# Low parts of q and V in the first batch made on GpSimd, with V scaled on ScalarE

## The chip, the cores and the metric

The kernel runs on one core of a Trainium2 chip. The metric is the device time of one execution in microseconds. The core has five engines, each with an instruction queue of its own that it works off in order: TensorE (PE in the profile, with PEld for the loading of weights), VectorE (DVE), ScalarE (ACT), GpSimd (POOL) and SyncE (SP), which here only issues DMA transfers. An instruction whose input isn't there holds up everything behind it in its own queue, and nothing else directly.

## The reference

What is computed is an attention over 2 batches of 8 heads with 768 positions of 64 numbers, in which a query sees only the keys that fall in its bucket (the signs of six random projections), and behind it two MLP layers on the 1536 tokens:

```python
mask = q_bucket[:, :, :, None] == k_bucket[:, :, None, :]
scores = scale * np.matmul(q, k.transpose(0, 1, 3, 2))
scores = np.where(mask, scores, -1000000000.0)
scores = scores - np.max(scores, axis=-1, keepdims=True)
attn = np.exp(scores)
attn = attn / (np.sum(attn, axis=-1, keepdims=True) + 1e-09)
out = np.matmul(attn, v)
...
h = x @ w_in                                  # both MLPs, 512 -> 2048 -> 512
g = h * (1.0 / (1.0 + np.exp(-1.702 * h)))    # the second MLP: without the 1.702
y = g @ w_out
```

## The kernel before

**Two parts for a number.** TensorE multiplies rounded numbers, so the kernel writes each float32 operand as a high part (the rounded number) and a low part (what the rounding lost) and multiplies the parts. A low part is a subtraction, `x - high`, on 128 partitions by 384 or 768 numbers. It is these subtractions that the change moves.

**Stages.** The attention runs over 96 steps: 16 heads, six blocks of 128 queries each. The first 48 steps are the first batch (`stage[0] == 0`), the rest the second batch, beside which the first MLP already works on the first batch's tokens (`stage[0] == 1`). From about 410 us on only the MLPs are left. In the trace of before the first batch's steps lie between some 13 and 150 us.

**One step j.** PE makes the scores in PSUM (`scores`, L404 and L405), DVE takes them out with the row's minimum (`top`, tile `p`, L422), ACT takes the exponential (`exps`, L427), ACT or in two of five steps of the first batch DVE rounds it to the high part (`p_high`, tile `hl`, L438 and L436), POOL makes its low part (`p_low`, L442). For every two steps SP issues one DMA that transposes both parts (`p_turn`, `pt<-hl`, L448), and PE multiplies them with V three steps behind (`av`, L460 to L462). `p` has three buffers in the first batch, the scores two, `hl` three.

**Preparing the next pair of heads.** Between the steps the function `ahead` places the pieces that prepare a pair of heads. For q and k of a head: a load by SP (L268, one buffer for each of q and k); `natural`, which makes the high part on DVE (L292) and the low part (L293) on the engine that `LOWG` names; `turn`, which transposes both on PE (L300); `evict` and `move`, which put them in place. For the V of a pair: a load by SP (`load_v`, L279, one buffer), the maximum on DVE (`v_max`, L364), a scale from it (`v_spread`, `v_scale`), the high part on ACT with that scale (`v_high`, L383) and the low part (`v_low`, L389 to L392). The buffer of q, k or V can be loaded anew only when the low part that reads it is done.

`LOWG` is a pair of strings, one for each batch; a letter in it puts the low part of that tensor on GpSimd. In `natural` the first two heads (n of 0 and 1) stay on DVE whatever `LOWG` says; `v_low` has no such exception. What is prepared in the first batch reaches two pairs ahead, so `stage[0] == 0` covers q of heads 0 to 10 and V of pairs 0 to 4.

**What sets the order.** The kernel is written as a program over tiles. A list scheduler with a time model of its own puts the instructions of each engine in their order before the kernel runs; the offsets in `SOONER` bring a named piece forward. The semaphores follow from the tiles' reads and writes.

Of the kernel before, what the change touches and what calls it, by code (L numbers as in the profile page):

```python
# [21 lines left out]
def tile_lsh_attention_two_mlps(  # L22
# [44 lines left out]
    EARLY = 0  # L67
    WSTART = 38
    WEVERY = 3
    LOWG = ('k', 'kqv')  # L70
    COPY = ('k', 'q')
    FB = 2
    PB = 2
# [175 lines left out]
    def attention(sp, s1, ps_m, ps_v, ahead_of, setup):  # L249
# [37 lines left out]
        def natural(n, nm):  # L287
            x = nat[n, nm]
            hp, lp = (1, 0) if nm == "q" else (0, 1)
            E = G if nm in LOWG[stage[0]] and n > 1 else V  # L290
            t = sp.tile([P, NC, 2, D], F32R, tag="s" + nm, name="s" + nm, bufs=1)
# [93 lines left out]
        def v_low(pr, j):  # L385
            vs, s = st["v", pr]
            x = nat[pr, "v"][:, j]
            if "v" in LOWG[stage[0]]:
                A.activation(x, x, AF.Copy, scale=s[:, j:j + 1])  # L389
# [378 lines left out]
```

## Time and profile before

| what | value |
|---|---|
| time, median of 3 runs (lowest to highest) | 832.61 us (831.09 to 833.43) |
| the profiled execution's own time | 831.93 us |
| its span, first to last instruction | 830.1 us |
| mean granted TensorE clock | 0.955 |
| busy: PE, DVE, POOL, ACT | 753.3, 533.9, 442.0, 421.4 us |
| from 20 to 150 us, busy: DVE, PE, ACT, POOL | 104.69, 100.58, 89.77, 83.54 of 130 us |

The profile is of one execution. Busy time is given per engine and per stretch; waits name the engine and line that an idle engine was waiting for; the chain is the work that ended last, followed back from the end, each piece with its start and length. A busy PE is not PE at its peak, and spans on POOL are rough.

### The profile page before, as it was taken

The page shows a single profiled execution, that of the slowest core. Times are in us where ns is not written, and L with a number is a line of the kernel's source. Part 1 is how long each engine was busy: PE and PEld are TensorE (multiplying, and loading weights), DVE is VectorE, ACT ScalarE, POOL GpSimd, SP SyncE. Part 2 cuts the span into 40 slices and gives each one's busy share as a digit, 9 for nine tenths or more (in the row PEclk, how much of TensorE's full clock was granted, in tenths as well). Part 3 has the DMA queues.
Part 4 walks back from the last instruction along what each step waited for, and adds up shares of the span by engine and source line. Part 5 has one row for each costly group of instructions (what it writes and reads, how often), then busy time and mean ns, then how long its engine had stood idle before and what let it go on. Part 6 is the DMA issues. An engine that isn't in the chain of part 4 may idle for free.

```text
span 830.1 us, 13998 instructions
## 1 busy us (share of the span) xinstructions
PE 753.3 (91%) x5384; PEld 692.9 (83%) x5384; DVE 533.9 (64%) x932; ACT 421.4 (51%) x721; POOL 442.0 (53%) x345
## 2 busy tenths in 40 slices
PE   6787787698898998988999999979999999999998
PEld 5677576577797887887999999979999989998996
DVE  8877787988689889779424233899733843422222
ACT  6758656596675666655534232444645433321220
POOL 5656676777777857766733242549534533421120
PEclk9778979599999999999999999999999999999999
DMA  4999999998998979865587421232310400000112
GB/s 117 190 180 193 200 180 223 231 247 238 246 254 231 223 216 226 210 153 109 108 300 261 150 104 49 77 127 95 108 51 21 132 2 1 0 1 1 39 39 76
DMA packets 196270, 116.40 MB, mean 140 GB/s; under 512 B 153318, under 2 KB 175846, under 8 KB 196204
## 3 DMA queue, kind: packets, MB, share of 16 engines
q1 hardware_dynamic: 196044, 115.52, 55.8%
q8 instruction: 42, 0.69, 0.3%
q14 instruction: 24, 0.20, 0.1%
q10 hardware_dynamic: 160, 0.00, 0.0%
HBM read 56.63 MB, written 16.78 MB: 88 GB/s over the span
## 4 chain that ended last, share of the span: by engine, by line
PE 59%; DVE 20%; DMA 10%; ACT 5%; issue 4%; POOL 1%; SPq 1%; DVEq 0%; ACTq 0%; POOLq 0%
PE pso L642 26%; PE psh L608 25%; DMA pt<-hl 6%; DVE f L173 3%; DVE p L422 3%; DVE f L171 3%; DVE f L175 2%; DVE f L172 2%; PE pss L404 2%; PE pss L405 1%; PE psbit L332 1%; POOL hl L442 1%; DMA nk<-in_k_dram 1%; PE pav L460 1%; ACT p L427 1%
## 5 line engine op out<-in xcount | busy, mean ns | idle before, releaser
L619 POOL TENSOR_TENSOR gl<-g,gh 128x384 fp32r<-128x384 f32 x128 | 138.3, 1081 | 201.7 <-ACT gh L618 189.5
L442 POOL TENSOR_TENSOR hl<-p,hl 128x768 f16<-128x768 f32 x96 | 168.0, 1757 | 75.7 <-ACT hl L438 33.2
L608 PE MATMUL psh<-XH,wih 128*128 128x384 f32 x512 | 174.2, 340 | 6.0 <-DVE part L651 3.9
L608 PE MATMUL psh<-XH,wil 128*128 128x384 f32 x512 | 173.0, 338 | 0.0
L608 PE MATMUL psh<-XL,wih 128*128 128x384 f32 x512 | 172.9, 338 | 0.0
L617 DVE TENSOR_TENSOR g<-g,psh 128x384 f32<-128x384 f32 x96 | 52.7, 550 | 116.8 <-ACT g L616 116.7
L651 DVE SCALAR_TENSOR_TENSOR part<-pso,part 128x384 f32<-128x384 f32 (+1 forms) x124 | 72.6, 590 | 83.0 <-PE pso L642 82.8
L427 ACT ACTIVATE p<-p,lo 128x768 f32<-128x768 f32 x96 | 89.7, 937 | 70.4 <-DVE p L422 70.2
L618 ACT CAST gh<-g 128x384 fp32r<-128x384 f32 x128 | 65.5, 512 | 86.7 <-DVE g L617 70.7
L608 PEld LDWEIGHTS psh<-XH,wih 128*128 128x128 f32 x512 | 97.2, 190 | 8.1 <-DVE g L614 2.2
L642 PE MATMUL pso<-gh,woh 128*128 128x384 f32 x256 | 88.6, 352 | 16.9 <-DVE g L614 7.0
L422 DVE TENSOR_SCALAR_CACHE_REDUCE p<-pss 128x768 f32<-128x768 f32 x96 | 90.8, 947 | 14.9 <-PE pss L405 8.6
L608 PEld LDWEIGHTS psh<-XL,wih 128*128 128x128 f32 x512 | 97.2, 190 | 0.6
L608 PEld LDWEIGHTS psh<-XH,wil 128*128 128x128 f32 x512 | 97.2, 190 | 0.0
L616 ACT ACTIVATE g<-psh 128x384 f32<-128x384 f32 x96 | 46.8, 488 | 96.2 <-PE psh L608 95.2
L404 PE MATMUL pss<-ak,aq 128*128 128x384 f32 x192 | 77.4, 404 | 19.7 <-DVE p L422 19.5
L642 PE MATMUL pso<-gl,woh 128*128 128x384 f32 x256 | 86.5, 338 | 0.0
L642 PE MATMUL pso<-gh,wol 128*128 128x384 f32 x256 | 86.5, 338 | 0.0
L460 PE MATMUL pav<-VS,pt 128*128 128x65 f16 x576 | 69.4, 205 | 15.4 <-DMA pt<-hl 13.0
L460 PEld LDWEIGHTS <-pt 128*128 128x128 f16 x576 | 57.4, 105 | 24.1 <-DMA pt<-hl 17.7
L642 PE MATMUL pso<-woh,gh 128*128 128x512 f32 x192 | 74.9, 390 | 0.2 <-ACT gh L618 0.2
L642 PE MATMUL pso<-wol,gh 128*128 128x512 f32 x192 | 75.0, 391 | 0.0
(114 smaller groups left out, 1623.1 us busy)
## 6 DMA issues: line engine op xcount, KB each, us to landing
raw<-in_moe_w_in_dram SPq DMA_DIRECT2D x32, 512.0 KB
raw<-in_moe_w_out_dram SPq DMA_DIRECT2D x32, 512.0 KB
spih<-wih SPq DMA_DIRECT2D x13, 256.0 KB
spil<-wil SPq DMA_DIRECT2D x13, 256.0 KB
spoh<-woh SPq DMA_DIRECT2D x13, 256.0 KB
spol<-wol SPq DMA_DIRECT2D x13, 256.0 KB
wih<-spih SPq DMA_DIRECT2D x13, 256.0 KB
wil<-spil SPq DMA_DIRECT2D x13, 256.0 KB
```

The lines of the kernel that those rows point to most:

```text
L404: T.matmul(o, lhsT=lq, rhs=ak[:, half, :], start=True, stop=False)
L422: V.tensor_scalar(p, st.pop(("S", j)), LOW, None, op0=ALU.min, op1=ALU.min, accum_out=lo)
L427: A.activation(p, p, AF.Exp, bias=lo, scale=-1.0)
L442: G.tensor_tensor(out=hl[:, 1], in0=st.pop(("p", j))[0], in1=hl[:, 0], op=ALU.subtract)
L460: T.matmul(o, lhsT=pt[:, i], rhs=hv, start=(i == 0), stop=False)
L608: T.matmul(h, lhsT=a[:, c], rhs=x[t][:, c], start=(n == 0), stop=(n == 3 * NDC - 1))
L616: A.activation(g, h, AF.Sigmoid, scale=beta)
L617: V.tensor_tensor(out=g, in0=g, in1=h, op=ALU.mult)
L618: A.copy(gh[:, f], g)
L619: G.tensor_tensor(out=gl[:, f], in0=g, in1=gh[:, f].bitcast(F32), op=ALU.subtract)
L642: T.matmul(y, lhsT=a, rhs=x, start=(n == 0), stop=(n == 3 * nf - 1))
L651: V.scalar_tensor_tensor(out=acc, in0=y, scalar=scale, in1=acc, op0=ALU.mult, op1=ALU.add)
```

## The change

The first batch's entry of `LOWG` becomes the same as the second's. The constants' line is all of the diff:

```diff
-    LOWG = ('k', 'kqv')
+    LOWG = ('kqv', 'kqv')
```

By it two places of the code take their other branch in the first batch:

```python
E = G if nm in LOWG[stage[0]] and n > 1 else V          # natural, L290: now also for q
...
if "v" in LOWG[stage[0]]:                               # v_low, L388
    A.activation(x, x, AF.Copy, scale=s[:, j:j + 1])    # scale V in place on ScalarE
    G.tensor_tensor(out=vs[:, j, :, D + 1:], in0=x, in1=vs[:, j, :, 0:D], op=ALU.subtract)
else:
    V.scalar_tensor_tensor(out=vs[:, j, :, D + 1:], in0=x, scalar=s[:, j:j + 1],
                           in1=vs[:, j, :, 0:D], op0=ALU.mult, op1=ALU.subtract)
```

The low part of q of heads 2 to 10 is then a subtraction on GpSimd. The low part of V of pairs 0 to 4, two instructions for each pair, is no longer one DVE instruction that scales and subtracts but a scaling on ScalarE and a subtraction on GpSimd. Since the scheduler runs again, the order of other instructions can change with it.

## Rows read from the trace of the kernel before

**Rows 1.** The page: busy tenths of DVE, and DMA, in 40 slices of 20.75 us.

```profile
DVE  8877787988689889779424233899733843422222
DMA  4999999998998979865587421232310400000112
```

**Rows 2.** Busy time by stretch: length, engines (instructions), granted clock, DMA share, GB/s.

```profile
20.00:150.00 130.00, 100.58 (x1089) 86.72 (x1090) 104.69 (x198) 89.77 (x131) 83.54 (x54) 0.83 0.99 193
...
220.00:240.00 20.00, 17.25 (x152) 16.20 (x150) 18.85 (x34) 10.22 (x16) 15.00 (x11) 0.91 1.05 273
```

**Rows 3.** Groups by line, 20 to 150 us: count, busy us, mean ns, idle before.

```profile
L442 POOL TENSOR_TENSOR hl<-p,hl 128x768 f16<-128x768 f32 x45 | 76.3, 1708 | 38.1 <-DVE hl L436 23.6 <-ACT hl L438 10.3 <-issue 4.1
L422 DVE TENSOR_SCALAR_CACHE_REDUCE p<-pss 128x768 f32<-128x768 f32 x45 | 42.4, 945 | 2.3 <-POOL hl L442 1.6 <-PE pss L405 0.7
...
L392 DVE SCALAR_TENSOR_TENSOR VS<-nv,sv,VS 128x384 f16<-128x384 f32 x9 | 11.4, 1266 | 0.0
L293 POOL TENSOR_TENSOR sk<-nk,sk 128x384 fp32r<-128x384 f32 x9 | 9.3, 1031 | 8.5 <-DVE sk L292 6.1 <-PE pstr L300 1.6 <-DVE sv L378 0.4
...
L293 DVE TENSOR_TENSOR sq<-nq,sq 128x384 fp32r<-128x384 f32 x8 | 8.2, 1031 | 0.1
```

**Rows 4.** Waits of the engines, 20 to 150 us: us in total, times, longest.

```profile
ACT p L427 <- DVE p L422: 25.2, 16, 4.7
POOL hl L442 <- DVE hl L436: 23.6, 16, 4.3
...
PEld L460 <- DMA pt<-hl: 11.7, 9, 3.8
DVE am L364 <- DMA nv<-in_v_dram: 9.8, 4, 4.2
...
PE pstr L300 <- POOL sk L293: 2.9, 1, 2.9
```

**Rows 5.** Waits of SP, the DMA queue's own, in the same stretch.

```profile
SPq L448 <- POOL hl L442: 54.3, 20, 3.8
SPq L268 <- DVE sq L293: 3.2, 3, 2.2
```

**Rows 6.** The chain that ended last: start us, length us, engine, tile, line.

```profile
18.77 2.01 DVE VS L392 x2
...
25.70 0.89 DVE sq L293
...
58.44 0.76 DVE VS L392
...
61.81 1.66 POOL hl L442
...
89.55 1.15 DVE sq L293
...
103.09 1.27 DVE VS L392
...
134.12 1.98 POOL hl L442
```

**Rows 7.** Single lines, 20 to 150 us: ns least/median/most, first and last start.

```profile
L392 DVE SCALAR_TENSOR_TENSOR VS<-nv,sv,VS x9: 609/1218/2102, 19.1 to 133.5; 128x384 f16<-128x384 f32 x9
L436 DVE CAST hl<-p x18: 517/550/1387, 22.2 to 143.5; 128x768 f16<-128x768 f32 x18
L292 DVE CAST sq<-nq x8: 332/805/1642, 24.0 to 123.2; 128x384 fp32r<-128x384 f32 x8
L422 DVE TENSOR_SCALAR_CACHE_REDUCE p<-pss x45: 918/944/959, 21.3 to 147.5; 128x768 f32<-128x768 f32 x45
```

**Rows 8.** Groups by line over the whole run: the same pieces in the second batch.

```profile
L293 POOL TENSOR_TENSOR sq<-nq,sq 128x384 fp32r<-128x384 f32 x5 | 6.0, 1196 | 1.8 <-DVE sq L292 1.5 <-DMA BK<-ak 0.3
L390 POOL TENSOR_TENSOR VS<-nv,VS 128x384 f16<-128x384 f32 x6 | 6.8, 1151 | 2.4 <-ACT nv L389 2.4
L389 ACT ACTIVATE nv<-nv,sv 128x384 f32<-128x384 f32 x6 | 3.6, 620 | 0.0
```

## The prediction

> **What bounds the kernel now.** The change acts on the first batch alone, so I read that stretch and not the whole. First the slices of the page [rows 1]: the first seven (to 145 us) have DVE at seven to eight tenths with DMA at nine, and from about 400 us on neither is full. The windows say the same in numbers [rows 2]: of the 130 us from 20 to 150, DVE is busy 104.69 (81%), PE 100.58, ACT 89.77 and POOL 83.54 (64%), and the DMA engines' share is 0.99. No engine is full; DVE and the DMA engines are nearest to it. Who waits for whom then decides [rows 4]. The longest waits end on DVE: ACT waits 25.2 us for L422, and POOL 23.6 us for the high parts that DVE rounds. DVE itself loses 9.8 us in four waits for V's load. The other side is the DMA queue [rows 5]: SP, which works off its queue in order, waits 54.3 us in 20 waits for POOL's p_low before it can issue a transposing DMA, and PE's weight loads wait 11.7 us for those transposes [rows 4]. So there are two paths side by side: DVE makes the material, and POOL hands it to SP. The change takes load from the first and puts it on the second.
>
> **What leaves DVE.** In the stretch nine scale-and-subtract instructions for V (11.4 us) and eight subtractions for q (8.2 us) leave it, 19.6 us [rows 3], and one of each just ahead of it. That is their full weight as traced, locks included. What of it lies on the path? The chain [rows 6] holds five pieces of this work: 2.01 + 0.89 + 0.76 + 1.15 + 1.27 = 6.1 us. All other instances stand where DVE's queue had slack. I take 6.1 us as the gain; its bounds are 0 (another path just as long runs beside) and 19.6 (DVE sets the pace throughout).
>
> **What it costs on POOL.** q's subtraction on POOL took 1.196 us in the second batch and V's 1.151 [rows 8]; the like of it for k took 1.031 us in the first batch [rows 3]. Eight by 1.03 and nine by 1.15 is 18.6 us, which takes POOL from 83.5 to 102.1 of 130 us (79%). POOL idles 38.1 us ahead of L442 [rows 3], and an instruction that falls into this costs nothing. If that cover is gone, it holds up the p_low behind it, and SP with that. The chain passes p_low in five pieces with six instructions, 9.8 us together (first and last in [rows 6]). Seventeen new instructions on 45 p_lows are 0.38 for each; by 1.1 us and six this is 2.5 us if each holds up in full, and 0 if none does. I take half, 1.2 us. The natural order of the queue behind a new instruction is p_low, then SP's transpose, and behind that SP's loads of q, k and V, so a late p_low delays those too; that is the third rival below.
>
> **What it costs on ACT.** Nine scalings by 0.620 us [rows 8] are 5.6 us. ACT waits 25.2 us for L422 in the stretch [rows 4], and that wait hides them: 0, at worst 5.6 us if they always stand ahead of an exponential that could start.
>
> **What PE and the loads see.** The turn of q now waits for POOL. For k this was one wait of 2.9 us on the matrix side in nine low parts [rows 4]; the same for eight q would be 2.6 us, against 0 where the scheduler leaves room. I take 0.5, since PE has 29 us idle here [rows 2]. V's buffer comes free after 0.62 us on ACT and 1.15 on POOL in place of 1.27 on DVE, 0.5 us later each time; the next V load, and DVE's reduction that waits for it (9.8 us in four [rows 4]), come later by that: 2.0 us, or with a p_low of 1.7 us [rows 3] ahead in POOL's queue, 8.8 us; below, the reduction may be ordered later and wait less, by at most the 9.8 us that it waits now. I take 0.5 us, near the point where the scheduler puts the reduction behind the new landing time. The load of q is freed by POOL and no longer by DVE, for which SP now waits 3.2 us [rows 5]; I put that even.
>
> **What it does to the rest of DVE.** The spread of single lines [rows 7] shows that DVE's instructions don't have one duration: V's low part took 0.609 to 2.102 us, q's high part 0.332 to 1.642, while L422, which reads PSUM, stays within 0.918 to 0.959. The stretched ones are those that read SBUF while POOL works. With POOL busy 1.22 times as long, the excess on those that remain grows. For the eight casts of q the excess of the median over the least is 0.47 us, 3.8 us; with the casts of k, put as alike, 7.6 us; a growth by 0.22 is 1.7 us. In the proportion in which DVE's work lies on the chain (6.1 of 19.6) this is 0.5 us; bounds 0 and 1.7.
>
> The Trainium skill, SBUF — State Buffer, section "Who interferes with whom", speaks against the change here: DVE and GpSimd share a port pair under an exclusive lock, and a DVE instruction in a two-port mode or with two SBUF inputs is fully blocked until the GpSimd instruction that came first has ended. The rows agree as to which lines are stretched. By the rule alone each of the 35 remaining casts (18 and 17) would meet one of the new POOL instructions with a chance of about 0.14 and wait half of 1.1 us or more, an estimate of 2.7 us and not 1.7; on the chain 0.8 and not 0.5, which moves the forecast by 0.3 us.
>
> **What comes after.** From 160 us on PE, DVE and the weights are shared with the MLP, and DVE is busier still (18.85 of 20 us from 220 to 240 [rows 2]). `LOWG` of that batch is unchanged and its order follows the attention's, so I carry what the first batch gains or loses to the end one for one. The order of instructions may change anywhere, since the scheduler works anew; the trace can't price this. The nearest row is the wait for V's load, 9.8 us, which a better order would save and a worse one would double; I take 0 and keep both signs for the range.
>
> **The sum.** -6.1 (DVE) + 1.2 (POOL ahead of p_low) + 0 (ACT) + 0.5 (PE) + 0.5 (V's load) + 0.5 (locks) = -3.4 us. From the profiled execution's 831.9 this gives 828.5; the median of the runs shown is 0.7 us higher than that execution, so I put the time at 829.0.
>
> **Rivals.**
> DVE alone sets the pace: all of the 19.6 us less 1.7 for locks comes back, 831.9 - 17.9 = 814.0. For it speak the waits for L422; against it, that only 6.1 us of this work is on the chain and that a DMA share of 0.99 leaves no room for a stretch shorter by 14%.
> The DMA engines set the pace: the first batch stays as long as it is and the freed DVE time becomes longer waits for loads and for `pt<-hl`, 831.9 within 2.5 us. For it speaks the share of 0.99; against it, that SP waits 54.3 us for POOL, so transposes go out when they are made and not when the engines are free, and that 273 GB/s were moved from 220 to 240 us against 193 here [rows 2], with other transfers. The case in which the change does nothing it says, because too few pieces are covered, ends here too; the counts speak against it.
> POOL becomes the bound ahead of p_low (slower): SP's wait for p_low is the largest of all, and each new subtraction of 1.1 us that stands in front of a p_low whose high part is ready goes through SP to the transposes, the loads behind them and DVE's waits for those loads. The point from which it decides is six such instructions on the chain (6.1 / 1.1); with twelve of the seventeen it costs 13.2 us, and less the 6.1 that DVE gives the end is 831.9 + 7.1 = 839.0. For it speaks that POOL is the engine that SP waits for; against it, its 38.1 us of idle time ahead of p_low.
>
> **How the numbers follow.** A change of less than 0.3% (2.5 us) can't be told from none here. The forecast, partial relief of DVE, gets 0.43 and has a range of its own from 822 to 829.4. DVE alone gets 0.04, DMA as the bound or nothing 0.25, POOL as the bound 0.28. So faster is 0.47, within 0.3% 0.25, slower 0.28. The range must take in the second and most of the third rival, with some of the order's 9.8 us on both sides: 820 to 841. It leaves out DVE alone and the far end of POOL's case, together about 0.1.
>
> **What would show it.** In the profile of the changed kernel, from 20 to 150 us or where the first batch then ends: DVE's busy time lower by some 18 us and no L392 in it; POOL at about 102 us; L293 on POOL for q at 1.0 to 1.2 us; ACT's wait for L422 clearly below 25 us if DVE was the bound. If SP's wait for p_low rises over 54 us, or POOL's idle time ahead of L442 goes to a few us while ACT and DVE wait for POOL, the slower rival is right. If DVE's waits for the loads of q, k and V and PE's for `pt<-hl` grow by what DVE lost in work, it is the DMA. The prediction is wrong in its ground if the first batch keeps its length while the second changes, since I carry the one into the other unchanged.

## The result, and the profile after

The changed kernel takes 839.91 us (median; 836.88 to 840.64) against 832.55 for the kernel before: a ratio of 1.0083, with a 95% interval of 1.0055 to 1.0112. It is slower by some 7 us, where 829.0 was forecast. The profiled execution of after is the quickest of its four (836.88 us); its span is 835.0 us, against 830.1, so its trace shows some 5 us of the loss.

The stretches first, as in [rows 2]: length, then busy time and instructions of PE, PE's weight loads, DVE, ACT and POOL, then granted clock, DMA share and GB/s. The kernel after, most of the first batch and most of the second:

```profile
20.00:150.00 130.00, 95.76 (x1092) 80.39 (x1092) 88.35 (x178) 92.94 (x141) 98.98 (x72) 0.89 0.99 193
155.00:430.00 275.00, 241.30 (x2089) 220.31 (x2089) 225.05 (x376) 174.64 (x285) 188.90 (x136) 0.96 0.84 202
```

The second stretch of the kernel before:

```profile
155.00:430.00 275.00, 244.56 (x2113) 225.15 (x2114) 218.70 (x382) 176.16 (x291) 190.57 (x139) 0.96 0.86 210
```

In the first batch the load moved nearly as forecast: DVE is busy 88.35 us for 104.69, POOL 98.98 for 83.54, ACT 92.94 for 89.77. (PE's 95.76 for 100.58 goes with a granted clock of 0.89 for 0.83; where the first batch is that of before, this stretch had from 0.82 in other_nudge to 0.87 in old_work_new_second, so I don't count it to the change.) In the second batch, which the diff doesn't touch, DVE is busy 6.4 us longer and does six instructions fewer in the same 275 us, and PE runs 24 matmuls fewer. So the second stretch falls behind.

The moved work in the first batch of after (groups by line as in [rows 3]: count, busy us, mean ns, idle before):

```profile
L442 POOL TENSOR_TENSOR hl<-p,hl 128x768 f16<-128x768 f32 x44 | 74.1, 1690 | 14.5 <-DVE hl L436 6.9 <-ACT hl L438 4.8 <-DVE sk L292 1.8
L390 POOL TENSOR_TENSOR VS<-nv,VS 128x384 f16<-128x384 f32 x10 | 10.1, 1007 | 0.0
L293 POOL TENSOR_TENSOR sq<-nq,sq 128x384 fp32r<-128x384 f32 x9 | 9.4, 1040 | 12.9 <-DVE sq L292 8.8 <-PE pstr L371 3.1 <-PE pss L405 0.6
L389 ACT ACTIVATE nv<-nv,sv 128x384 f32<-128x384 f32 x10 | 6.0, 607 | 0.0
```

Nineteen instructions of 1.0 us are now on POOL and ten of 0.61 us on ACT. POOL's idle time ahead of L442 fell from 38.1 to 14.5 us. The waits of the engines there (us in total, times, longest), to be held against [rows 4]:

```profile
ACT p L427 <- DVE p L422: 24.3, 16, 6.0
PEld L460 <- DMA pt<-hl: 23.3, 13, 4.4
PE pav L460 <- DMA pt<-hl: 19.9, 11, 4.3
DVE am L364 <- DMA nv<-in_v_dram: 8.1, 3, 4.2
POOL hl L442 <- DVE hl L436: 6.9, 10, 1.8
```

And those of SP's queue, beside [rows 5]:

```profile
SPq L448 <- POOL hl L442: 27.7, 9, 5.3
SPq L448 <- POOL VS L390: 10.2, 3, 5.0
SPq L448 <- POOL sk L293: 10.0, 3, 3.8
SPq L448 <- POOL sq L293: 8.0, 2, 4.3
```

POOL's wait for the rounded parts dropped from 23.6 to 6.9 us, but ACT's wait for L422 is where it was (24.3 for 25.2), and PE's weight loads wait 23.3 us for the transposed parts (`pt`) where they waited 11.7. SP's four waits on POOL ahead of the transposes add up to 55.9 us; in before the two there are 54.3 [rows 5] and 2.9. A wait for one engine became one for another. What this costs is not to be read from the rows; the runs below say it.

### The profile page after: what moved, and what is told of

Its sections match the earlier page's. It is cut to its first block, busy times and chain, and to the rows that moved or that the text cites. A ratio compares the mean times of both kernels' runs of the same rounds, so it can differ in the third digit from the quotient of the medians.

```text
span 835.0 us, 14042 instructions
## 1 busy us (share of the span) xinstructions
PE 750.4 (90%) x5384; PEld 687.2 (82%) x5384; DVE 524.2 (63%) x913; ACT 427.4 (51%) x731; POOL 460.0 (55%) x364
## 4 chain that ended last, share of the span: by engine, by line
PE 57%; DVE 17%; DMA 14%; ACT 5%; issue 5%; POOL 1%; SPq 1%; DVEq 0%; POOLq 0%; ACTq 0%
PE pso L642 26%; PE psh L608 25%; DMA pt<-hl 8%; DVE f L173 3%; DVE p L422 3%; DVE f L171 2%; DVE f L175 2%; DVE f L172 2%; DMA raw<-in_moe_w_out_dram 2%; DMA nk<-in_k_dram 1%; ACT p L427 1%; PE psbit L332 1%; ACT f L170 1%; DMA raw<-in_moe_w_in_dram 1%; PE pss L404 1%
## 5 line engine op out<-in xcount | busy, mean ns | idle before, releaser
L619 POOL TENSOR_TENSOR gl<-g,gh 128x384 fp32r<-128x384 f32 x128 | 140.3, 1097 | 198.9 <-ACT gh L618 186.7
L442 POOL TENSOR_TENSOR hl<-p,hl 128x768 f16<-128x768 f32 x96 | 166.8, 1741 | 53.1 <-ACT hl L438 25.1
L422 DVE TENSOR_SCALAR_CACHE_REDUCE p<-pss 128x768 f32<-128x768 f32 x96 | 90.9, 948 | 15.0 <-PE pss L405 13.1
L460 PE MATMUL pav<-VS,pt 128*128 128x65 f16 x576 | 66.2, 201 | 28.9 <-DMA pt<-hl 28.6
L404 PE MATMUL pss<-ak,aq 128*128 128x384 f32 x192 | 75.3, 393 | 14.9 <-DVE p L422 13.6
L460 PEld LDWEIGHTS <-pt 128*128 128x128 f16 x576 | 55.5, 101 | 39.9 <-DMA pt<-hl 36.1
```

The source lines that it names most:

```text
L404: T.matmul(o, lhsT=lq, rhs=ak[:, half, :], start=True, stop=False)
L422: V.tensor_scalar(p, st.pop(("S", j)), LOW, None, op0=ALU.min, op1=ALU.min, accum_out=lo)
L442: G.tensor_tensor(out=hl[:, 1], in0=st.pop(("p", j))[0], in1=hl[:, 0], op=ALU.subtract)
L460: T.matmul(o, lhsT=pt[:, i], rhs=hv, start=(i == 0), stop=False)
L619: G.tensor_tensor(out=gl[:, f], in0=g, in1=gh[:, f].bitcast(F32), op=ALU.subtract)
```

## The experiments

The compiler's scheduler orders the instructions of each engine anew for every program, so a plain comparison of two kernels mixes two things: other work, and another order of all the rest. Most runs below separate them. The recorded order of one kernel is laid on the other by edges that say "not before this one" between successive instructions of an engine; they add no semaphore and no work. The edit, at the program's end, shortened:

```diff
+    for engine in ORDER:                      # recorded places in the program
+        last = None
+        for c in engine:
+            if not (True): continue           # "c >= edge": from the second batch on
+            i = at[c]
+            if last is not None:
+                tc.add_manual_dep(i, last.name, NoSync, reason="pin")
+            last = i
```

The moved pieces themselves (L293, L389, L390, L392 of the first batch) are left out of it and go where the scheduler puts them; only in the last two runs, low_parts_out and short_low_parts, do they stand at their old place too. No run holds a kernel in its own order; that several held kernels come out at 831 to 832 us says that the edges alone cost little. All ratios are to the kernel before; a run's own kernel before, timed beside it, had medians of 831.86 to 832.69 us.

### Work or order: four combinations

**move_old_order**: the kernel after, in the whole order of before.

> The work of the kernel after (19 low parts on GpSimd, 10 scalings on ScalarE), but every other instruction of each engine is held in the order that it has in the kernel before, over the whole run; only the moved pieces go where the scheduler puts them. Theory A (the loss is the new order of the instructions, and the move itself gives a little): 826 to 831 us. Theory B (the move itself costs, since GpSimd's queue holds up p_low and the transposes): 838 to 842 us. Theory C (the move is even and the order is all of the loss): 831 to 834 us.

835.83 us, 1.0043 (1.0028 to 1.0058): between the ranges of the three theories.

**old_work_new_order**: the kernel before, in the whole order of after.

> The counterpart: the low parts of q and V are made on VectorE as in the kernel before, but every other instruction stands in the order of the kernel after. Theory A: above the kernel after, 842 to 848 us, since the order's loss stays and the move's gain is gone. Theory B: 830 to 835 us. Theory C: 838 to 842 us.

838.96 us, 1.008 (1.0059 to 1.01). The old work in the new order costs as much as the change.

**move_old_second**: the kernel after with its own first batch; from the second batch on (`c >= edge`) in the order of before.

> The kernel after, with its own order for the first batch; what is written for the second batch and the MLPs stands in the order of the kernel before. The first batch of after ended 0.6 to 3 us late by the 48th to 51st step, and most of its lag arose between 200 and 300 us. Theory A with the loss in the second batch's order: 830 to 835 us. Theory B: 837 to 842 us, as after. If it is still at 838 or more, the loss sits in the first batch or in the passage between the two.

832.01 us, 0.9992 (0.9976 to 1.0009).

**old_work_new_second**: the kernel before with its own first batch; from the second on in the order of after.

> The kernel before with its own order for the first batch; what is written for the second batch and the MLPs stands in the order of the kernel after. Theory A with the loss in the second batch's order: 837 to 842 us although nothing was moved. Theory B: 831 to 834 us.

839.89 us, 1.0085 (1.0064 to 1.0106).

Together they make a table (us):

| | second batch in before's order | second batch in after's order |
|---|---|---|
| first batch of before | 832.5 (before) | 839.9 |
| first batch of after | 832.0 | 839.9 (after) |

The rows are equal, the columns 7.4 to 7.9 us apart. The whole loss comes from the order that the scheduler gave to the second batch and the MLPs, and the first batch of after, its own order and the moved work together, costs nothing and gains nothing. That the kernel after is slow although its moved work isn't: this settles it. The run move_old_order shows a second thing, taken up below: in before's order of the first batch, the move does cost 3.7 us.

**other_nudge**: the kernel before with one number of the scheduler changed and nothing moved.

```diff
-    SOONER = ({..., 'p_turn': 35, ...
+    SOONER = ({..., 'p_turn': 50, ...
```

> The kernel before with nothing moved: only the scheduler's offset for the transposing DMA in the first batch is 50 instead of 35, which changes the order in the first batch from its third pair on and everything in the second. If the order in the second batch is worth several us whatever it was that changed it, this is 2 to 10 us away from the kernel before, more likely above it (835 to 842 us); if only the moved parts make a worse order, it is at 831 to 834 us.

836.21 us, 1.0052 (1.0035 to 1.007). An edit that changes no work at all moves the time by 4.4 us: an order made anew can cost something of this size by itself.

### What in the second order costs it

The most visible trace of it was on DVE: its four weight lines in the second stretch (groups by line), the kernel before:

```profile
L173 DVE SCALAR_TENSOR_TENSOR f<-raw,f 128x512 int32<-128x512 int32 x31 | 34.2, 1105 | 0.4
L175 DVE SCALAR_TENSOR_TENSOR f<-raw,f 128x512 int32<-128x512 int32 x31 | 29.7, 959 | 0.2
L171 DVE TENSOR_SCALAR f<-f 128x512 f32<-128x512 f32 x30 | 26.1, 871 | 11.4 <-ACT f L170 11.4
L172 DVE TENSOR_SCALAR f<-f 128x512 int32<-128x512 int32 x30 | 21.8, 730 | 0.3
```

The kernel after:

```profile
L175 DVE SCALAR_TENSOR_TENSOR f<-raw,f 128x512 int32<-128x512 int32 x30 | 35.7, 1189 | 0.3
L173 DVE SCALAR_TENSOR_TENSOR f<-raw,f 128x512 int32<-128x512 int32 x30 | 35.4, 1179 | 0.4
L172 DVE TENSOR_SCALAR f<-f 128x512 int32<-128x512 int32 x30 | 28.1, 937 | 0.5
L171 DVE TENSOR_SCALAR f<-f 128x512 f32<-128x512 f32 x30 | 22.1, 737 | 9.5 <-ACT f L170 9.3
```

The same instructions take 121.3 us and not 111.8. A reading of this is that in the new order they fall beside POOL's work more often. Against it stands other_nudge, which loses 4.4 us with 112.6 us on these lines. If they are the cause, the old order on DVE and POOL alone must bring the time back.

**old_second_dve_pool**: the kernel after; the second batch in before's order on DVE and POOL only (`ORDER` of those two engines, `c >= edge`).

> The kernel after; what is written for the second batch and the MLPs stands in the order of the kernel before on VectorE and GpSimd only, and the scheduler orders the other engines. Four runs so far have the second batch at a loss of 4 to 9 us with VectorE's four lines for the weights (L171 to L175) at 121 us in 155 to 430 us, and at none with 109 to 112 us. Theory H (the order of VectorE against GpSimd decides, by the locks): 831 to 834 us with those lines at 109 to 114 us. Theory I (the order of the matmuls or of the DMA queue decides): 837 to 841 us.

843.27 us, 1.0126 (1.0099 to 1.0154): slower than either. Its weight lines:

```profile
L173 DVE SCALAR_TENSOR_TENSOR f<-raw,f 128x512 int32<-128x512 int32 x30 | 29.9, 996 | 0.3
L171 DVE TENSOR_SCALAR f<-f 128x512 f32<-128x512 f32 x30 | 28.6, 952 | 10.2 <-ACT f L170 10.2
L175 DVE SCALAR_TENSOR_TENSOR f<-raw,f 128x512 int32<-128x512 int32 x30 | 27.9, 930 | 0.2
L172 DVE TENSOR_SCALAR f<-f 128x512 int32<-128x512 int32 x30 | 22.5, 754 | 0.2
```

They are short again (108.9 us), and the time is the longest of all. Shortening the weight lines is thus not enough to bring the time back. Since this mixed order has losses of its own, the run doesn't show that the lines cost nothing in after. What grew here is PE's wait for the transposes (waits of PE in this run's second stretch; the first line reads 3.4 us in before and 7.7 in after):

```profile
PE pav L460 <- DMA pt<-hl: 17.5, 11, 4.0
PE psh L608 <- DVE g L614: 4.7, 1, 4.7
```

**old_second_pe_act_sp**: the kernel after; the second batch in before's order on PE, ACT and SP only.

> The kernel after; the second batch and the MLPs in the order of the kernel before on TensorE, ScalarE and the DMA queue only, VectorE and GpSimd as the scheduler orders them. Theory H: 836 to 841 us with the four lines for the weights at 117 us or more. Theory I: 831 to 834 us.

837.0 us, 1.0063 (1.0041 to 1.0086). This half brings back 2 us, if anything (the intervals of 1.0063 and 1.0083 overlap). The time is where Theory H put it, but the weight lines take 113.4 us and not the 117 or more that it asked for. Of the divisions tried, only all five engines together give 832.0. This suggests that the engines' orders have to fit one another.

The traces show where the loss arises. From 200 to 250 us (columns as above) the kernel before, the kernel after and old_work_new_second:

```profile
200.00:250.00 50.00, 44.88 (x375) 40.94 (x372) 38.32 (x74) 36.19 (x62) 35.56 (x27) 0.97 1.03 247
200.00:250.00 50.00, 42.89 (x320) 39.71 (x320) 41.65 (x66) 32.10 (x55) 32.34 (x25) 0.97 0.90 234
200.00:250.00 50.00, 43.51 (x317) 41.00 (x318) 41.91 (x67) 31.85 (x56) 31.83 (x24) 0.93 0.88 233
```

From 20 to 200 us the three have 1496, 1486 and 1483 matmuls. In these 50 us the two with after's order of the second batch fall behind by 55 and 58. DVE's wait for a load of k there, in the same three:

```profile
DVE sk L292 <- DMA nk<-in_k_dram: 1.9, 1, 1.9
DVE sk L292 <- DMA nk<-in_k_dram: 4.7, 1, 4.7
DVE sk L292 <- DMA nk<-in_k_dram: 4.4, 1, 4.4
```

While DVE stands at L292, the L422 behind it in its queue can't start, and ACT's longest wait for L422 is 5.1 us in the last two against 2.6 in before. The wait is 4.4 to 4.8 us in all three traces with after's whole order in the second batch, and 1.9 to 3.3 us in all with before's whole order there. So the place of k's high part in DVE's queue is a candidate. It is at most 3 us of the 7, other_nudge loses its 4.4 us without it (its wait is 2.0 us), and no run tests it: which waits make up the 7 us stays open.

### What the move itself does: the order held

**q_old_order**: only q moves, in the order of before.

```diff
-    LOWG = ('k', 'kqv')
+    LOWG = ('kq', 'kqv')
```

> Only q's nine low parts go to GpSimd; everything else in the order of the kernel before. The move of both in that order took 835.8 against 832.2. Theory F (the cost is V's: its buffer comes free only after GpSimd's queue, SP then holds up everything behind V's load): 829 to 832 us. Theory G (the cost is GpSimd's load as such, and each part has its share): 833 to 835 us.

831.36 us, 0.9986 (0.9968 to 1.0004). Moving q costs nothing and may save 1 us.

**v_old_order**: only V moves (`('kv', 'kqv')`), in the order of before.

> Only V's ten low parts go to GpSimd, scaled on ScalarE; everything else in the order of the kernel before. Theory F: 835 to 838 us, with SP waiting some 10 us for these low parts ahead of V's loads and VectorE's wait for V's load at 18 to 20 us instead of 9.8. Theory G: 833 to 835 us.

840.86 us, 1.0099 (1.0076 to 1.0123): above the ranges of both theories. V alone costs 8.2 us. Its wait of DVE, and the one of SP's queue that goes with it, from 20 to 150 us:

```profile
DVE am L364 <- DMA nv<-in_v_dram: 15.2, 5, 4.4
```

```profile
SPq L279 <- POOL VS L390: 9.1, 3, 5.6
```

The same queue at that line in before:

```profile
SPq L279 <- DVE sk L292: 1.3, 1, 1.3
SPq L279 <- DVE VS L392: 0.8, 1, 0.8
SPq L279 <- DVE p L422: 0.7, 2, 0.5
```

L279 is the load of V. In before, SP waits 2.8 us at it in all and never for POOL, and DVE waits 9.8 us for V [rows 4]. The move lets V's buffer `nv` go only when GpSimd has read it, and GpSimd's queue is busy; SP stands at the load for up to 5.6 us, with everything behind it in its queue. In move_old_order SP's wait there is 10.3 us and DVE's 19.7, longer than here, and yet that run loses only 3.7 us: the wait alone doesn't give the size of the loss, and why moving q as well makes it smaller stays open. The test of the cause: free the buffer from ScalarE.

**v_own_tile_old_order**: V moves as in v_old_order, but ScalarE writes the scaled V of the first batch into a tile of its own and GpSimd reads that (the diff shortened).

```diff
-                A.activation(x, x, AF.Copy, scale=s[:, j:j + 1])
-                G.tensor_tensor(out=vs[:, j, :, D + 1:], in0=x, in1=vs[:, j, :, 0:D], op=ALU.subtract)
+                w = sp.tile([P, NC, D], F32, tag="vy", name="vy", bufs=1)
+                A.activation(w, x, AF.Copy, scale=s[:, j:j + 1])
+                G.tensor_tensor(out=vs[:, j, :, D + 1:], in0=w, in1=vs[:, j, :, 0:D], op=ALU.subtract)
```

> Only V's ten low parts are moved, as in the run that took 840.9, in the order of the kernel before; but ScalarE writes the scaled V of the first batch to a tile of its own, so that V's buffer comes free after ScalarE and not after GpSimd. Theory F (V's 9 us come from the late release of its buffer): 830 to 834 us, and SP's wait for these low parts ahead of V's loads gone from 9 us. Theory J (GpSimd's extra instructions ahead of p_low are the cost): 837 to 841 us, as before.

830.85 us, 0.9989 (0.9972 to 1.0006). From 1.0099 to 0.9989 is 1.1%, some 9 us, by one tile. The two waits in its trace, which is of the slowest of its twelve executions (837.02 us):

```profile
DVE am L364 <- DMA nv<-in_v_dram: 8.9, 5, 3.5
SPq L279 <- ACT vy L389: 1.3, 1, 1.3
```

SP no longer waits for POOL at V's load, so the late release of V's buffer is the likely cost. One thing isn't separated from it: the scheduler placed the free pieces anew, and six of the ten subtractions of V now stand one or two p_lows earlier in POOL's queue.

**both_own_tile_old_order**: q and V moved, V through its own tile, in the order of before.

> Both moved, V scaled to a tile of its own, the order of the kernel before. With V's buffer held by GpSimd this took 835.8 against 832.2. Theory F: 829 to 832 us, no better than the 829.7 of the run without these low parts. Theory J: 834 to 838 us.

829.42 us, 0.9967 (0.9951 to 0.9983): faster than both kernels, by 2.7 us against before. Its stretch from 20 to 150 us, DVE's wait for V, and SP's wait at V's load:

```profile
20.00:150.00 130.00, 94.83 (x1107) 82.56 (x1108) 90.62 (x182) 95.19 (x143) 101.18 (x72) 0.88 1.00 196
```

```profile
DVE am L364 <- DMA nv<-in_v_dram: 10.7, 5, 4.2
```

```profile
SPq L279 <- ACT vy L389: 1.3, 1, 1.3
```

DVE and POOL carry about the loads of the kernel after, and the wait for V is back at the 10 us of before.

**both_own_tile_second**: the same work with the scheduler's own first batch, the second batch in before's order.

> Both moved, V scaled to a tile of its own; the first batch in the order that the scheduler finds for it, the second batch and the MLPs in the order of the kernel before. With V scaled in place this was 832.0 against 832.2. Theory F: 828 to 831 us; Theory J: 831 to 834 us.

834.73 us, 1.0033 (1.0013 to 1.0053): just above Theory J's range, and slower than before.

**q_old_second**: only q moved, likewise.

> Only q's nine low parts are moved; the first batch in the order that the scheduler finds for it, the second batch and the MLPs in the order of the kernel before. With all in the order of before it was 831.4 against 831.9. If the first batch's own order lets VectorE's relief come through: 828 to 831 us; if loads and transposes pace it: 831 to 833 us.

834.61 us, 1.0013 (0.9992 to 1.0033). That, too, is above what was expected. With its own order in the first batch each kernel is ordered anew: beside the 832.0 of move_old_second, the version with V's own tile is 2.7 us slower, and q alone is 2 to 3 us slower than in the held order, though the intervals of these two overlap. So the tile of its own is no gain here, and what V's release does can't be told from what the order does.

### What DVE's work was worth

**low_parts_out**: in the first batch V's low parts and those of q of heads 2 to 9 are left out and replaced by an operation on two numbers of the same input, so that buffers come free as before; in the order of before. The DVE time of that work is taken away, and POOL gets none of it. The edit for q (the one for V is alike):

```diff
+            V.tensor_reduce(out=TINY1[:, 0:1], in_=x[:, 0, 0:2], axis=AX.X, op=ALU.max)
```

> Left out: in the first batch the low parts of V (all ten) and of q (heads 2 to 9), which are zero. In their place VectorE reduces two numbers of the same input, so that the buffers come free at the same place; all orders are those of the kernel before. In the run with the low parts cut to one column these instructions still took 0.99 us (V) and 0.73 us (q) in the mean, so VectorE was relieved of some 7 us only; here it is relieved of some 17 us, since a reduction doesn't wait for GpSimd. Theory D (VectorE sets the pace, 6 us or more to be had): 822 to 827 us. Theory E (loads and transposes pace the first batch): 829 to 832 us.

829.69 us, 0.9963 (0.9943 to 0.9982): 3.0 us. Its first stretch, V's line there (ns least/median/most, first and last start) and two of its waits:

```profile
20.00:150.00 130.00, 100.44 (x1132) 87.40 (x1132) 89.13 (x199) 91.13 (x134) 85.10 (x55) 0.85 1.01 198
```

```profile
L392 DVE TENSOR_REDUCE TINY<-nv x8: 134/148/152, 33.3 to 131.2; 128x1 f32<-128x2 f32 x8
```

```profile
PEld L460 <- DMA pt<-hl: 16.3, 12, 2.8
PE pav L460 <- DMA pt<-hl: 12.5, 10, 2.7
```

In before the second line reads

```profile
PE pav L460 <- DMA pt<-hl: 9.6, 6, 3.6
```

and the first 11.7 us [rows 4]. DVE is rid of 15.6 us, and 3.0 come back in the end; PE waits 4.6 and 2.9 us longer for the transposes, and the DMA share is 1.01. This fits a part of the freed time having turned into waits for transfers; no run tests that by itself.

**short_low_parts**: the same low parts stay on DVE but are cut to one of 64 columns (6 elements for each partition), in the order of before; the other columns are not computed. The edit for q, shortened (the one for V is alike):

```diff
-            E.tensor_tensor(out=t[:, :, lp], in0=x, in1=t[:, :, hp].bitcast(F32), op=ALU.subtract)
+            E.tensor_tensor(out=t[:, :, lp, 0:1], in0=x[:, :, 0:1], in1=t[:, :, hp, 0:1].bitcast(F32), op=ALU.subtract)
```

> Left out: in the first batch the low parts of V (all ten) and of q (heads 2 to 9) are subtracted over one column of 64 only and are zero in the others; they stay on VectorE, at their place, and every instruction of every engine stays in the order of the kernel before. So VectorE is relieved of some 18 us of its work without anything put on GpSimd or ScalarE and without a later release of a buffer. Theory D (VectorE's work on the chain is worth what the prediction said): 824 to 827 us, and down to 815 if VectorE alone sets the pace. Theory E (the first batch is paced by loads and transposes that land, and VectorE's freed time turns into waits for them): 830 to 833 us.

831.56 us, 0.9995 (0.9979 to 1.001): no change that can be measured. DVE was relieved of less than expected: from 20 to 150 us it is busy 96.43 us for 104.69. The two lines from 20 to 150 us (ns least/median/most, first and last start):

```profile
L392 DVE SCALAR_TENSOR_TENSOR VS<-nv,sv,VS x8: 240/1217/1734, 34.4 to 132.0; 128x6 f16<-128x6 f32 x8
```

```profile
L293 DVE TENSOR_TENSOR SQ<-nq,SQ x7: 160/641/1489, 25.7 to 111.0; 128x6 fp32r<-128x6 f32 x7
```

One sixty-fourth of the work has a median of 1.217 us on V's line, the same as the whole (1.218 [rows 7]); the mean is 0.990 us against 1.266 [rows 3], and the least is 0.240. The time line shows what the long ones do:

```profile
34.44 0.24 DVE L392 SCALAR_TENSOR_TENSOR VS<-nv,sv,VS 128x6 f16<-128x6 f32 x1
35.25 1.66 POOL L442 TENSOR_TENSOR hl<-p,hl 128x768 f16<-128x768 f32 x1 [2.01 <-ACT hl L438]
35.46 1.49 DVE L392 SCALAR_TENSOR_TENSOR VS<-nv,sv,VS 128x6 f16<-128x6 f32 x1
```

The first L392 ran while POOL was idle. The second began 0.21 us after a p_low and ended 0.04 us after it. So most of what V's low part costs on DVE beside POOL is waiting for POOL. The Trainium skill, SBUF — State Buffer, section "Who interferes with whom", says that a VectorE instruction with two SBUF inputs contends with a GpSimd instruction that reads SBUF, and that the one issued first holds the shared ports for its whole length while the other is blocked. These lines agree. Making the instruction smaller saved little of this time; giving it another form did: the operation with one small input in low_parts_out took 0.134 to 0.152 us, beside POOL too, and that run is 3.0 us quicker.

## Why the prediction was wrong, step by step

- **The order, put at 0: this step failed.** I took the change of order as nothing, since the trace can't price it, and wrote that the second batch's "order follows the attention's, so I carry what the first batch gains or loses to the end one for one". It doesn't: the second batch was scheduled anew though nothing in it was touched, and that alone is 7.4 us (839.9 with the old work in the first batch, 839.9 with the new, against 832.5 and 832.0). The range took some of the order's 9.8 us on both sides and so reached the result; the chances did not weigh it.
- **DVE's relief, 6.1 us: too large by two.** The five pieces on the chain were real, but with that work gone altogether 3.0 us come back (low_parts_out). That the other instances stood where DVE had slack was read off one chain, and 3.0 us is less than even its pieces. The waits that grew are those for the transposes, so a second path hardly shorter, that of the transfers, is the likely reason; it is not shown.
- **POOL ahead of p_low, 1.2 us: nothing that can be measured.** With the order held and V's buffer freed early, moving the work (0.9967) is within 0.04%, 0.3 us, of leaving it out (0.9963), but each has an interval of 0.16 to 0.2% on either side, so 1.2 us isn't excluded. POOL's idle time ahead of L442 fell by 23.6 us in after, more than the 19.5 us of new work there.
- **V's load, 0.5 us: mis-sized, but only seen with the old order.** In before's order V's own tile takes away some 9 us where V alone is moved (1.0099 against 0.9989) and some 6 where q is moved too (1.0043 against 0.9967). The first is near the 8.8 that I named for a p_low ahead of V's low part in POOL's queue. In after the wait for V is 8.1 us, below the 9.8 of before; there it is not seen.
- **ACT, 0, and PE, 0.5:** nothing speaks against them. ACT's own time rose 3.2 us, and moving q costs nothing in the held order (0.9986). The sign that I named for DVE as the bound, ACT's wait for L422 clearly below 25 us, did not come: 24.3 for 25.2 us.
- **Locks on the rest of DVE, 0.5 us:** the 35 casts of L436 and L292 took 25.8 us in before and 26.7 in after, 0.9 us more, where I had 1.7 and 2.7. What of this lies on the path isn't separated from the rest.
- **The sum, -3.4 us:** with before's order held, the move as the diff makes it costs 3.7 us, so the sum has the wrong sign even without the order. It gives -2.7 us only with V's own tile, which the kernel after doesn't have; that this is near -3.4 is luck, a gain half as large less costs near nothing. The last step of the sum has a slip too: 828.5 and 0.7 is 829.2, not 829.0.
- **The second rival describes the first batch of after best.** With the second batch's order held the time is 832.0, as that rival has it, and PE's weight loads wait 11.6 us longer for transposes, where DVE lost 16.3 us of work. That the DMA engines are what binds isn't shown by this: SP's waits for POOL ahead of the transposes are as long as before.
- **Two readings of [rows 1] were loose**, without weight in the sum: the first slice has DMA at four tenths, and DVE is at eight to nine again in slices from some 520 to 580 us.
- **The third rival had the right sign for another reason.** It wanted SP's wait for p_low above 54 us; it fell to 27.7, and the first batch as a whole is even (832.0 with the second batch's order held). The time, 839.0, is near the result by accident. What did come true is the last sentence on what would make the prediction wrong in its ground: the first batch keeps its length while the second changes. (In the traces the first batch's last L422, the 48th, starts at 152.6 us in after and at 147.5 in before; the 51st, in the second batch, at 163.9 and 164.1. The lag is made up there.)

Open: which wait in the new order of the second batch takes the 7 us. By old_second_dve_pool shorter weight lines are not enough, and neither of the two groups of engines whose order was put back alone gives the time back. DVE's wait for a load of k between 200 and 250 us is a candidate for a part of it.

## What to carry to other kernels

Where a scheduler orders the program, an edit in one stage redraws the order of all others, and here that was worth more (0.5 and 0.9%) than the edit: lay the old order on the new work and the new order on the old work before you explain a small difference, and put the order into the chances as a case of its own. When an operation moves to a busy in-order engine, ask first whose buffer it now frees and which load waits for that; a tile of its own for the intermediate was worth 6 to 9 us with the order held, and nothing where the scheduler ordered the first batch itself. And don't take an engine's work on the chain of waits for what its removal gives: here 6.1 us on the chain gave 3.0.

## What the runs showed of the hardware

A VectorE scale-and-subtract of 6 elements for each partition, with two inputs in SBUF, took 1.217 us at the median and 0.240 at the least in a stretch in which GpSimd was busy two thirds of the time (short_low_parts). Where it was long, it ended with GpSimd's instruction. A reduction of 2 elements with one input in SBUF stayed at 0.134 to 0.152 us (low_parts_out). L422, which reads PSUM, stayed at 0.917 to 0.958 us in after, with POOL's load a fifth higher. That two orders of the same instructions in the second batch, with the same work in the first (before and old_work_new_second), lie 0.9% apart at a granted clock of 0.96 and 0.95 in the second stretch was more than I had expected.
